# DeltaNet with a low-rank mixer on one core: the first batch's recurrence takes U into PSUM, its z goes through ScalarE, and the written-out order is new from there

## The chip, the core and the metric

The kernel runs on one core of a Trainium2 chip. Five engines work side by side, each through its own queue and in order: TensorE (PE) multiplies matrices into the accumulation memory PSUM, VectorE (DVE) and ScalarE (ACT) work elementwise and bring PSUM back into SBUF, GpSimd (POOL) clears tiles and issues some transfers, SyncE (SP) issues the others. Semaphores join them. The metric is the device time of one launch in microseconds, lower is better, as the median of several runs.

## The reference

Two blocks follow each other. The first is a delta rule, for 4 batches, 8 heads, 768 tokens and head size 48:

```python
k_n = k / (norm(k) + 1e-06)
for t in range(S):
    y[t]  = q[t] @ state
    v_old = state.T @ k_n[t]
    state = state + beta[t] * outer(k_n[t], v[t] - v_old)
```

The second takes the heads side by side as x (4 x 768 x 384):

```python
u   = x + (x.T @ U @ V).T              # over the tokens, rank 32
out = u + relu(u @ w_ch1) @ w_ch2      # 384 -> 1536 -> 384
```

U and V of this second block are weights. The U of the change is another thing: a term of the first block, below.

## The kernel before

The recurrence is not run token by token. A batch is cut into 12 chunks of 64 tokens, and six chunks make a unit n, so that batch b has units 2b and 2b + 1 and there are eight units. For each unit the kernel builds Gram matrices of k and q (`grams`, with `turn`, `placed` and `products`), inverts a triangular system by substitution on VectorE (`blocks`, steps of L842 and L848), and joins the small inverses into 64 x 64 ones on TensorE (`joins`, `part`, `diagonals`). Units 0 and 1 use a form with a halved substitution and larger joining matmuls (L899, L913).

With the inverse T of a chunk the recurrence over the chunks is short. Let S be the state, K the chunk's keys. Then U = T V holds the corrected values without the state, W = T K the corrected keys, z = U - W S, the output is y = Q S + (masked Q K) z, and the next state is S + K z. `prepare(n, h)` makes W for three chunks. `recur(b)` runs the twelve chunks in turn: one group of matmuls for W S (called b), z, one group for K z (s), and the addition to S on VectorE (L1214, L1216 for the first chunk). `outputs` makes y in two groups (L1024 and L1038) and copies it to X (L1008).

There are two ways to make z, and the constant JOINT chooses by batch. For b < JOINT, `prepare` also multiplies U (L1083), copies it to SBUF (L1096), and z is the subtraction U - W S on VectorE, out of PSUM (L1182). For b >= JOINT, `prepare` copies W with its sign turned, a part `values(c)` multiplies U of one chunk into a pair of PSUM banks, the group b adds -W S into the same place, and ScalarE copies the sum as z (L1160). The other half of that pair later takes the product for the next state. JOINT is 1, so that only batch 0 goes the first way.

The weights come as 64-bit floats, in 14 slices numbered 0 to 13. SyncE starts each slice as two transfers (`start`), ScalarE scales its upper words (`raised`, L1301), and VectorE puts the 32-bit numbers together in three steps (`load_weights`, L1315, L1322, L1329). The staging buffers are reused, so that a later slice starts only when an earlier one has been decoded.

When all chunks of batch 0 have their outputs, `front` makes u in strips of 256 tokens (L1574, L1580, L1588, L1593, L1609, L1621), `channels` multiplies by w_ch1 (L1683), and `narrow` by w_ch2 (L1861). From there on the mixer of one batch runs beside the preparation and the recurrence of the next.

All these parts are generators, and each `yield op(...)` is a step. What stands next on which queue is not left to a scheduler: ORDER, a text of some 2,500 numbers, lists for each part the positions of its steps, and `run` resumes the parts in this order. An engine's queue holds its own steps in order of their positions. Costs given to `op` decide nothing here.

For the steps that follow it matters where they stand. Before the change, with positions of ORDER: `recur b0` runs from 244 (the matmuls of the first state) to 474; `prepare n0 h1` stands at 211 to 223, `prepare n0 h0` at 227 to 233, `prepare n1 h0` at 356 to 369 and `prepare n1 h1` at 370 to 402; the joining steps of unit 1 lie between 232 and 335; the scalings of slices 6 to 13 stand at 363, 381, 384, 415, 432, 507, 505 and 575; the first `channels` step stands at 546. The names s0 to s10 below are the state additions of chunks 0 to 10 of batch 0, z1 to z11 its z.

Of the kernel before, what the change touches and what calls it, by code (L numbers as in the profile page):

```python
# [27 lines left out]
def kernel(  # L28
# [33 lines left out]
    NU = 2  # L62
# [82 lines left out]
    add_up b0 i0 f00: 607 626 632; add_up b0 i0 f03: 613 616 625; add_up b0 i1 f00: 858 866 891; add_up b0 i1  # L145
    f03: 853 867 874; add_up b0 i2 f00: 1070 1075 1083; add_up b0 i2 f03: 1094 1098 1102; add_up b1 i0 f00: 1305
    1309 1322; add_up b1 i0 f03: 1303 1316 1328; add_up b1 i1 f00: 1487 1488 1500; add_up b1 i1 f03: 1486 1497
    1501; add_up b1 i2 f00: 1708 1711 1720; add_up b1 i2 f03: 1709 1721 1723; add_up b2 i0 f00: 1859 1861 1863;
    add_up b2 i0 f03: 1860 1862 1864; add_up b2 i1 f00: 1999 2003 2012; add_up b2 i1 f03: 2002 2008 2011; add_up
    b2 i2 f00: 2224 2225 2227; add_up b2 i2 f03: 2226 2228 2230; blocks n0: 61 73 75 76 82 84 86 88 89 91 93 94  # L150
    96 97 103 110 114 122; blocks n1: 143 157 160 163 173 175 179 192 201 206 208 212 213 215 218 219 226 229;
    blocks n2: 479 509 512 515 517 519 521 528 532 535 538 540 543 545 549 551 554 558; blocks n3: 648 661 678
    680 682 693 701 706 707 716 717 721 725 734 736 738 749 753 755 760 763 770 771 773 787 788 789 790 799 801
    810 811 812 813; blocks n4: 957 971 973 974 975 986 988 990 991 998 1003 1005 1018 1019 1030 1057 1065 1069
    1071 1073 1076 1078 1082 1084 1085 1088 1090 1097 1099 1103 1108 1117 1129 1133; blocks n5: 1164 1187 1195
    1199 1218 1223 1226 1249 1258 1262 1276 1286 1291 1304 1307 1318 1330 1335 1337 1345 1347 1352 1358 1362
    1368 1372 1374 1380 1382 1389 1391 1403 1404 1410; blocks n6: 1535 1560 1566 1569 1577 1578 1579 1595 1596
    1597 1610 1611 1624 1630 1632 1647 1657 1665 1668 1672 1674 1687 1697 1707 1726 1728 1731 1738 1745 1748
    1751 1764 1773 1779; blocks n7: 1829 1853 1868 1869 1870 1873 1875 1884 1893 1895 1898 1901 1905 1909 1920
    1925 1926 1936 1937 1946 1950 1956 1969 1972 1975 1988 1994 1996 2000 2004 2014 2015 2020 2022; channels b0  # L160
    i0 e0: 546 547; channels b0 i0 e1: 556 557; channels b0 i0 e2: 562 563; channels b0 i0 e3: 565 566; channels
    b0 i0 e4: 580 582; channels b0 i0 e5: 599 601; channels b0 i1 e0: 708 709; channels b0 i1 e1: 727 741;
    channels b0 i1 e2: 754 756; channels b0 i1 e3: 758 781; channels b0 i1 e4: 797 807; channels b0 i1 e5: 808
    837; channels b0 i2 e0: 987 989; channels b0 i2 e1: 1000 1001; channels b0 i2 e2: 1020 1025; channels b0 i2
    e3: 1053 1054; channels b0 i2 e4: 1061 1062; channels b0 i2 e5: 1079 1087; cut f0 f00 k0 to1: 2338; cut f0
    f00 k1 to0: 2316; cut f0 f00 k1 to1: 2333; cut f0 f00 k2 to0: 2347; cut f0 f00 k2 to1: 2361; cut f1 f03 k0
    to1: 2369; cut f1 f03 k1 to0: 2429; cut f1 f03 k1 to1: 2372; cut f1 f03 k2 to0: 2409; cut f1 f03 k2 to1:
    2418; cut f2 f06 k0 to1: 2325; cut f2 f06 k1 to0: 2362; cut f2 f06 k1 to1: 2337; cut f2 f06 k2 to0: 2346;
    cut f2 f06 k2 to1: 2357; cut f3 f09 k0 to1: 2395; cut f3 f09 k1 to0: 2416; cut f3 f09 k1 to1: 2396; cut f3
    f09 k2 to0: 2417; cut f3 f09 k2 to1: 2421; diagonals n0 h0: 188 190 191 195 210 222; diagonals n0 h1: 167  # L170
    169 171 176 181 186; diagonals n1 h0: 312 315 319 336 343 353; diagonals n1 h1: 290 292 303 338 349 358;
    diagonals n2 h0: 628 649 660 667 686 696; diagonals n2 h1: 665 684 689 711 723 730; diagonals n3 h0: 820 821
    830 833 841 842; diagonals n3 h1: 878 905 907 908 925 956; diagonals n4 h0: 1153 1163 1166 1197 1244 1245;
    diagonals n4 h1: 1216 1231 1233 1267 1287 1289; diagonals n5 h0: 1416 1421 1433 1434 1435 1440; diagonals n5
    h1: 1450 1505 1537 1555 1556 1587; diagonals n6 h0: 1823 1890 1891 1913 1914 1915; diagonals n6 h1: 1843
    1872 1878 1889 1906 1911; diagonals n7 h0: 2041 2055 2071 2080 2112 2121; diagonals n7 h1: 2044 2048 2078
    2139 2144 2151; fifteen b1 i0 k0: 1176 1181 1186 1212 1232 1243 1274; fifteen b1 i0 k1: 1160 1178 1183 1211
    1225 1240 1256 1273; fifteen b1 i1 k0: 1394 1398 1406 1426 1455 1464 1468; fifteen b1 i1 k1: 1371 1396 1402
    1420 1431 1448 1458 1465; fifteen b1 i2 k0: 1581 1598 1613 1628 1639 1662 1675; fifteen b1 i2 k1: 1576 1588
    1605 1614 1631 1640 1654 1670; fifteen b2 i0 k0: 1762 1777 1789 1805 1820 1832 1848; fifteen b2 i0 k1: 1758  # L180
    1765 1778 1803 1806 1819 1830 1847; fifteen b2 i1 k0: 1921 1933 1953 1962 1967 1979 1984; fifteen b2 i1 k1:
    1910 1930 1934 1951 1961 1964 1978 1983; fifteen b2 i2 k0: 2088 2111 2135 2146 2163 2198 2213; fifteen b2 i2
    k1: 2089 2119 2130 2145 2162 2166 2178 2190; front b0 i0: 495 497 504 511 526 537; front b0 i1: 542 555 614
    629; front b0 i2: 845 859 862 863; front b1 i0: 1060 1077 1080 1089 1095 1114; front b1 i1: 1265 1275 1313
    1315; front b1 i2: 1478 1480 1499 1506; front b2 i0: 1688 1694 1699 1710 1724 1735; front b2 i1: 1839 1854
    1866 1888; front b2 i2: 1945 1948 2007 2029; front b3 i0: 2214 2215 2216 2219 2221 2229; front b3 i1: 2232
    2233 2237 2238; front b3 i2: 2240 2242 2245 2246; gather b0 i0 h0 c0 k0: 623; gather b0 i0 h0 c0 k1: 633;
    gather b0 i0 h0 c1 k6: 705 934; gather b0 i0 h1 c0 k2: 655; gather b0 i0 h1 c0 k5: 715 1171; gather b0 i0 h1
    c1 k3: 666; gather b0 i0 h1 c1 k4: 681; gather b0 i1 h0 c0 k0: 876; gather b0 i1 h0 c0 k1: 911; gather b0 i1
    h0 c1 k6: 970 1126; gather b0 i1 h1 c0 k2: 920; gather b0 i1 h1 c0 k5: 964 977; gather b0 i1 h1 c1 k3: 919;  # L190
    gather b0 i1 h1 c1 k4: 942; gather b0 i2 h0 c0 k0: 1100; gather b0 i2 h0 c0 k1: 1109; gather b0 i2 h0 c1 k6:
    1169 1609; gather b0 i2 h1 c0 k2: 1131; gather b0 i2 h1 c0 k5: 1159 1321; gather b0 i2 h1 c1 k3: 1135;
# [486 lines left out]
    def grams(n, i):  # L679
# [46 lines left out]
        def products(j, i):  # L726
# [3 lines left out]
            for c in range(UC):  # L730
                for par, g in QUADS:
# [5 lines left out]
                        start=True,  # L737
# [256 lines left out]
    JOINT = 1  # L994

    def recur(b):
# [127 lines left out]
        zs = {}  # L1124
        if b >= JOINT:
            for c in range(NC):
# [992 lines left out]
```

## Time and profile before

| | |
|---|---|
| median of 3 runs | 579.35 us (577.87 to 580.1) |
| the profiled execution | 579.14 us, its span 577.4 us |
| TensorE busy | 544.6 us, 94% of the span |
| VectorE busy | 466.7 us, 81% |
| ScalarE busy | 252.0 us, 44% |
| GpSimd busy | 133.5 us, 23% |
| mean granted clock of TensorE | 0.939 |
| moved by DMA | 36.26 MB |

The times to predict are medians of unprofiled runs. The profile is one execution; its span runs from the first to the last instruction, and 1.7 us of the execution's own time lie around it. A row of a timeline gives the start, the time taken, the engine, the line, the operation, and what is written from what, in what size; "x16" is the number of merged instructions, and a bracket at the end the idle time before it and what ended it. Each fp32 matmul of the program stands as two instructions. The granted clock is the share of TensorE's full clock that the chip gave it. The matmuls overlap, so that the distance from start to start is what a group costs on the queue, not its length.

### The profile page before, as it was taken

To read this page: it belongs to the slowest core of one execution; us is meant where nothing else is said; L and a number is where in the kernel's file an instruction comes from. 1 tells how busy PE (TensorE), PEld (TensorE's weight loads), DVE (VectorE), ACT (ScalarE), POOL (GpSimd) and SP (SyncE) were. 2 spreads that over 40 slices of the span, in tenths; PEclk is the share of its full clock that TensorE was granted. 3 is DMA by queue.
4 is the path that set the end of the run, shared out by engine and by line. 5 is a ranking of instruction groups with operands and counts; after the bars stand their busy time and mean duration, and the time that the engine had idled before them with its cause. 6 is when DMAs were issued, how large, how long until landed. Compare 5 with 4: busy or idle time off the path is not lost.

```text
span 577.4 us, 24113 instructions
## 1 busy us (share of the span) xinstructions
PE 544.6 (94%) x10692; PEld 482.3 (84%) x10692; DVE 466.7 (81%) x1100; ACT 252.0 (44%) x528; POOL 133.5 (23%) x229
## 2 busy tenths in 40 slices
PE   3878888899999999999999999999999999999997
PEld 3777876588988986998999998989999978755996
DVE  3888768899999789999996799989995435799942
ACT  2846565644435542266154643264345461345000
POOL 9122026205124430072222262061002000000000
PEclk9665557999999999999999999999999999999999
DMA  9980628643022243131501523060003000000001
GB/s 144 182 183 26 221 69 196 140 85 65 20 51 43 48 77 63 30 85 36 98 10 20 102 58 82 2 128 19 3 2 85 5 3 1 28 0 1 1 27 69
DMA packets 89399, 36.26 MB, mean 63 GB/s; under 512 B 75408, under 2 KB 87056, under 8 KB 89296
## 3 DMA queue, kind: packets, MB, share of 16 engines
q1 hardware_dynamic: 80752, 24.69, 20.7%
q0 software_dynamic: 6944, 9.74, 7.9%
q8 instruction: 84, 1.38, 1.0%
q10 hardware_dynamic: 1600, 0.30, 0.3%
q14 instruction: 19, 0.16, 0.1%
HBM read 29.98 MB, written 4.72 MB: 60 GB/s over the span
## 4 chain that ended last, share of the span: by engine, by line
PE 83%; DVE 7%; ACT 4%; issue 2%; DMA 2%; SPq 1%; DVEq 0%; ACTq 0%
PE P L1861 21%; PE P L1721 15%; PE P L1683 9%; PE P L1988 7%; PE P L1488 7%; PE P L733 3%; PE P L1024 2%; PE P L1114 2%; PE P L1146 2%; PE P L913 2%; PE P L1064 2%; PE P L1038 2%; PE P L899 2%; PE P L1609 1%; PE P L1588 1%
## 5 line engine op out<-in xcount | busy, mean ns | idle before, releaser
L1861 PE MATMUL P<-w_sb,hs 128*128 128x192 f32 x540 | 94.4, 329 | 0.0
L1861 PEld LDWEIGHTS P<-w_sb,hs 128*128 128x128 f32 x540 | 87.2, 190 | 2.6 <-issue 1.8
L848 DVE TENSOR_TENSOR xt<-xt,prod 128x112 f32<-128x112 f32 (+21 forms) x200 | 64.6, 323 | 6.9
L842 DVE TENSOR_TENSOR prod<-gs,xt 128x112 f32<-128x112 f32 (+21 forms) x200 | 62.8, 314 | 2.2
L1721 PE MATMUL P<-S,w_sb 128*128 128x128 f32 x432 | 56.6, 282 | 0.0
L1721 PEld LDWEIGHTS P<-S,w_sb 128*128 128x128 f32 x432 | 51.5, 191 | 2.6 <-DVE xt L848 0.6
L1683 PE MATMUL P<-ut,w_sb 128*128 128x256 f32 x216 | 51.4, 388 | 0.0
L1750 DVE TENSOR_TENSOR hs<-hs,P 128x512 f32<-128x512 f32 x54 | 36.5, 682 | 11.8 <-PE P L1721 10.4
L1683 PEld LDWEIGHTS P<-ut,w_sb 128*128 128x128 f32 x216 | 39.6, 190 | 7.4 <-issue 1.8
L588 POOL DMA_DIRECT2D slot<-in_v_dram x32 | 21.2, 669 | 102.2 <-DVE X L1788 46.8
L1008 ACT COPY X<-P 64x192 f32<-64x192 f32 x96 | 30.0, 313 | 22.0 <-PE P L1038 19.4
L985 POOL MEMSET slot<- 32x384 f32 x32 | 13.1, 412 | 107.6 <-PE P L942 101.9
L1160 ACT COPY z<-P 128x192 f32<-128x192 f32 x36 | 11.4, 318 | 60.4 <-PE P L1146 52.1
L1861 PE MATMUL P<-w_sb,S 128*128 128x192 f32 x216 | 37.7, 329 | 0.0
L1861 PEld LDWEIGHTS P<-w_sb,S 128*128 128x128 f32 x216 | 34.9, 190 | 0.8 <-issue 0.6
L978 ACT COPY slot<-zz 32x384 f32<-32x384 f32 x64 | 32.3, 509 | 4.3 <-DVE zz L917 3.3
L1744 ACT ACTIVATE hs<-P 128x512 f32<-128x512 f32 x30 | 17.8, 597 | 36.5 <-PE P L1721 32.9
L733 PE MATMUL P<-slot 48*64 48x64 f32 x1536 | 30.9, 233 | 0.7 <-DVE slot L770 0.7
L588 POOL DMA_DIRECT2D slot<-in_k_dram x44 | 29.7, 678 | 7.9 <-PE P L1202 7.6
L733 PEld LDWEIGHTS P<-slot 48*64 48x64 f32 x1536 | 27.7, 146 | 4.0 <-issue 1.5
L574 POOL DMA_DIRECT2D slot<-in_k_dram x40 | 24.6, 622 | 11.3 <-PE P L1202 6.5
L1214 DVE TENSOR_TENSOR s<-s,P 128x192 f32<-128x192 f32 x40 | 14.0, 349 | 14.7 <-PE P L1202 10.9
(208 smaller groups left out, 1197.4 us busy)
## 6 DMA issues: line engine op xcount, KB each, us to landing
w_sb<-in_moe_w_ch_dram SPq DMA_DIRECT2D x10, 384.0 KB, 5.4
out_dram<-X SPq DMA_DIRECT2D x19, 192.0 KB, 2.8
slot<-in_k_dram SPq DMA_DIRECT2D x48, 72.0 KB, 3.5
slot<-in_k_dram POOLq DMA_DIRECT2D x44, 72.0 KB, 3.4
slot<-in_v_dram SPq DMA_DIRECT2D x32, 72.0 KB, 3.1
slot<-in_v_dram POOLq DMA_DIRECT2D x32, 72.0 KB, 2.9
X<-in_moe_w_ch_dram SPq DMA_DIRECT2D x6, 384.0 KB, 5.0
wide<-in_moe_w_ch_dram SPq DMA_DIRECT2D x6, 384.0 KB, 5.7
```

The source lines that it names most:

```text
L588: queue.dma_start(out=t[half(1 - g if name == "z" else g), :, to, 0:D], in_=src[b, 4 * g + s, hf * UC * L : (hf + 1) * UC * L, :].rearrang ...
L733: nc.tensor.matmul(p_g[half(g ^ (par * i)), par, c], kq[rows, c, j, 0, half(g)], kq[rows, c, j, i, half(g)], start=True, stop=True,)
L842: nc.vector.tensor_tensor(out=prod, in0=gb[:, :, j : j + 1, j + 1 :].to_broadcast([128, split, m, w]), in1=xb[:, :, 0:m, j : j + 1].to_bro ...
L848: nc.vector.tensor_tensor(out=xb[:, :, 0:m, j + 1 :], in0=xb[:, :, 0:m, j + 1 :], in1=prod, op=ALU.subtract,)
L978: nc.scalar.copy(pg[quarter(i), :, at, :, a : a + BK], cut(zc, h)[quarter(i)].rearrange("p r (c j) t -> p r c j t", j=2),)
L1008: nc.scalar.copy(x[half(c % 2), c // 2, 4 * D * g : 4 * D * (g + 1)].rearrange("p (j r d) -> p r j d", r=2, d=D), states(p_y)[half(g)],)
L1488: nc.tensor.matmul(to, forms[h][w][:, g] if isinstance(w, str) else w1_of(*w, h)[:, g], TOKENS[t] if isinstance(t, str) else u_of(*t), sta ...
L1683: nc.tensor.matmul(p_f[:, x], w(x, t), ut[:, t], start=(t == 0), stop=(t == KT - 1))
L1721: nc.tensor.matmul(p[:, g], forms[h][w][:, g % 2] if isinstance(w, str) else w1_of(*w, h)[:, g % 2], PLACES[int(t[1:])] if isinstance(t, s ...
L1750: nc.vector.tensor_tensor(out=to, in0=to, in1=p, op=ALU.add if sign > 0 else ALU.subtract)
L1861: nc.tensor.matmul(to, of[0], of[1], start=of[2], stop=of[3], skip_group_check=True)
L1988: nc.tensor.matmul(p[:, m], a[:, h, 128 * m : 128 * m + 128], v[:, h, j], start=fresh and h == j == 0 and (m == 0 or apart), stop=(j == h ...
```

## The change

JOINT becomes 0, so that batch 0 too goes the second way: `values` for its twelve chunks, the b group added into PSUM, z copied by ScalarE. Two conditions in `products` that were written with JOINT keep their meaning as plain numbers (n > 2 and n <= 2; before, NU * JOINT was 2).

```diff
@@ products @@
-                if n > NU * JOINT:
+                if n > 2:
...
-                for r in range(2) if n <= NU * JOINT else ():
+                for r in range(2) if n <= 2 else ():
@@ ahead of recur @@
-    JOINT = 1
+    JOINT = 0
```

ORDER has five steps more: `values b0` brings twelve, `recur b0` one (the z of the first chunk), and the four `prepare` of units 0 and 1 lose two each. Up to position 204 it is as before. From 205 to 1097 it is new: other positions for nearly all parts, those of batch 0's recurrence, unit 1's joins, the weight slices, units 2, 3 and the beginning of 4, batch 0's mixer and batch 1's recurrence. From 1098 on (1093 before) it is the former one with all numbers five higher. The positions that the prediction speaks of, in place of the full text:

```diff
-prepare n0 h0: 227 228 231 233; prepare n0 h1: 211 214 221 223
-prepare n1 h0: 356 366 368 369; prepare n1 h1: 370 376 394 402
+prepare n0 h0: 230 235; prepare n0 h1: 234 239
+prepare n1 h0: 351 360; prepare n1 h1: 412 422
+values b0 c0 to c11: 229 237 263 290 318 332 366 385 395 405 423 463
-joins n1 h0: 254 267 279 284 287 293 295 297 298 307 308 313 325 327 328 335
-joins n1 h1: 232 234 236 239 247 258 268 271 281 285 286 289 302 304 305 324
+joins n1 h0: 228 253 254 255 269 270 275 276 277 283 284 289 291 293 296 300
+joins n1 h1: 231 249 259 260 304 307 313 319 324 340 341 342 378 390 397 399
-recur b0: 244 249 250 264 266 270 273 283 300 306 310 316 322 331 332 337 342
-  344 347 348 362 365 371 373 374 377 378 387 396 399 404 405 410 413 417 424
-  426 429 436 445 463 465 471 474
+recur b0: 236 241 242 256 257 265 268 272 288 303 306 308 316 320 333 336 343
+  349 350 355 367 369 377 382 383 393 394 396 400 402 407 409 413 419 426 429
+  433 437 440 441 446 465 466 470 484
-load_weights, from the fourth: 225 241 245 251 255 269 272 282 288 291 301 311
-  330 333 339 364 375 379 392 401 409 422 425 430 431 433 439 450 452 508 516
-  518 520 530 552 560 581 585 597
+load_weights, from the fourth: 232 243 245 246 271 274 278 279 280 301 302 305
+  314 325 344 345 348 352 358 368 375 384 386 387 391 404 406 408 417 420 425
+  439 456 458 459 460 489 527 542
-raised i3 to i13: 262 278 320 363 381 384 415 432 507 505 575
+raised i3 to i13: 252 264 298 330 335 359 379 398 418 455 483
-products n2 i0 (first steps): 449 455; turn n2 i0: 440 443
+products n2 i0 (first steps): 468 490; turn n2 i0: 450 464
-outputs b0 c0: 240 253 259 ... outputs b0 c11: 466 476 480 481
+outputs b0 c0: 238 240 250 ... outputs b0 c11: 469 496 497 498
-front b0 i0: 495 497 504 511 526 537; channels b0 i0 e0: 546 547
+front b0 i0: 502 506 519 520 522 530; channels b0 i0 e0: 531 532
```

In `recur b0` before, the numbers are in turn PE and VectorE for the first chunk (s, the copy of the state), and then b, z, s, addition for each further one. After, the first chunk has z, s, copy, and each further one b, z (now ScalarE), s, addition. In `joins` of unit 1 the second, third, fifth and sixth numbers are the diagonal steps, the 10th, 11th, 13th and 14th the off-diagonal ones on PE.

On SyncE's queue the starts of slices 3 and 4 go ahead of unit 1's v, and the later slices ahead of the loads of unit 2's k and q. On GpSimd's queue two loads of unit 1's v (209, 210) go ahead of two clearings of unit 0 (214, 215; before, 210 and 222).

More of the change, by code (lines that the diff above doesn't have):

```diff
@@ L180 @@
[L180 to L189, printed above, removed]
```

460 lines of the change are left out of this document (236 added, 224 removed).

## The prediction

> **What bounds the kernel now.** I read the page first, then the stretches of 4 us, then who waited for whom between 44 and 116 us, then single instructions. The page gives busy time and share of the span for TensorE (PE) and VectorE (DVE), the granted clock in 40 slices of 14.4 us, and the chain that ended last:
>
> ```profile
> PE 544.6 (94%) x10692; PEld 482.3 (84%) x10692; DVE 466.7 (81%) x1100; ACT 252.0 (44%) x528; POOL 133.5 (23%) x229
> PEclk9665557999999999999999999999999999999999
> PE 83%; DVE 7%; ACT 4%; issue 2%; DMA 2%; SPq 1%; DVEq 0%; ACTq 0%
> ```
>
> PE is busy for 94% and carries the chain, and its clock is low only in the first seven slices. The stretches (from:to, length, then busy us of PE, PEld, DVE, ACT, POOL, the granted clock, DMA share, GB/s) show where it still idles:
>
> ```profile
> 36.00:40.00 4.00, 4.00 (x80) 4.00 (x79) 3.26 (x9) 1.82 (x5) 0.54 (x1) 0.50 1.11 219
> 68.00:72.00 4.00, 2.74 (x64) 2.74 (x66) 0.16 (x1) 1.15 (x3) 0.00 (x0) 0.50 0.73 243
> 84.00:88.00 4.00, 3.76 (x164) 3.60 (x156) 0.88 (x2) 3.90 (x8) 2.81 (x5) 0.58 0.43 91
> 88.00:92.00 4.00, 2.65 (x143) 2.27 (x136) 3.62 (x8) 2.98 (x5) 3.40 (x6) 1.00 0.92 169
> 96.00:100.00 4.00, 3.54 (x71) 2.91 (x64) 3.93 (x6) 2.17 (x5) 3.75 (x7) 0.50 0.94 196
> 116.00:120.00 4.00, 4.00 (x21) 3.51 (x20) 3.71 (x15) 0.65 (x2) 0.00 (x0) 1.00 0.89 220
> ```
>
> From 116 us PE is full at full clock. There a new order of the same matmuls can only lose. What the edit can gain lies between about 50 us and the mixer's first matmul (L1683 below), where PE has gaps and mostly half clock. The anchors there are DVE's copies of the state S: s0 (L1216), s4 and s5 (L1214), s10 (L1214). After them come the front's copy (L1580) and the first mixer matmul (columns: start, us, engine, line, operation):
>
> ```profile
> 59.84 0.34 DVE L1216 COPY s<-P 128x192 f32<-128x192 f32 x1
> 80.49 0.35 DVE L1214 TENSOR_TENSOR s<-s,P 128x192 f32<-128x192 f32 x1
> 85.92 0.34 DVE L1214 TENSOR_TENSOR s<-s,P 128x192 f32<-128x192 f32 x1
> 103.66 0.34 DVE L1214 TENSOR_TENSOR s<-s,P 128x192 f32<-128x192 f32 x1
> 109.07 0.56 DVE L1580 COPY tt<-P 128x384 f32<-128x384 f32 x1
> 114.46 2.86 PE L1683 MATMUL P<-ut,w_sb 128*128 128x256 f32 x12
> ```
>
> **The change, part by part.** First its arithmetic, by groups (all of the span for L1160, 48 to 116 us for the others):
>
> ```profile
> L1160 ACT COPY z<-P 128x192 f32<-128x192 f32 x36 | 11.4, 318 | 60.4 <-PE P L1146 52.1
> L1182 DVE TENSOR_TENSOR z<-slot,P 128x192 f32<-128x192 f32 x11 | 3.8, 348 | 4.7 <-PE P L1169 4.3 <-ACT X L1008 0.4
> L1096 ACT COPY slot<-P 128x576 f32<-128x576 f32 x4 | 2.6, 638 | 0.6 <-PE P L1083 0.6
> L1083 PE MATMUL P<-slot 64*64 64x48 f32 x192 | 5.7, 277 | 0.0
> L957 PE MATMUL P<-zz 32*32 32x32 f32 x72 | 2.6, 238 | 2.0 <-ACT X L1008 1.1 <-ACT zz L947 0.9
> ```
>
> - DVE loses 11 subtractions, 3.8 us. ScalarE (ACT) gains 12 z copies of 318 ns, 3.8 us, and loses four copies of U, 2.6 us. One z on the chain costs 318 instead of 348 ns: 0.03 us times 11, nothing.
> - PE loses the U products of prepare (192 matmuls, 5.7 us) and gains twelve groups of the same 16 matmul rows each, `values`. Below I price a group at 0.46 us, which gives 5.5 us. Equal. The minus sign rides on a copy that is there anyway, and the conditions n > 2 and n <= 2 decide as before. Cost nil.
> - One pair of PSUM banks per chunk now serves z and S, held from `values` on, where two were taken. Nothing in the trace prices it; I take 0, with at most one 0.7 us wait (such as those of the front below) as an upper end and none as the lower.
>
> So the work is equal, and the order decides. I price PE's queue between s0 and s10 in both orders with these rows of the half clock, and two rows of full clock (102.82, 103.04) for comparison:
>
> ```profile
> 64.16 0.70 PE L1169 MATMUL P<-s,slot 48*64 48x48 f32 x16
> 64.62 0.66 PE L1038 MATMUL P<-z,slot 64*64 64x48 f32 x16
> 65.08 1.43 PE L899 MATMUL P<-zz,hs 64*64 64x16 f32 x24
> 97.94 1.54 PE L705 MATMUL P<-ident,slot 128*128 128x128 f32 x6
> 101.12 1.89 PE L733 MATMUL P<-slot 48*64 48x64 f32 x96
> 102.82 0.40 PE L1024 MATMUL P<-s,slot 48*64 48x48 f32 x16
> 103.04 0.36 PE L1202 MATMUL P<-z,slot 64*48 64x48 f32 x16
> ```
>
> From start to start a group of the recurrence (b, S, both halves of y, `values`) is 0.46 us, at full clock 0.22. A diagonal step of unit 1's joins is 1.43, an off-diagonal one 0.4 (six in the L957 row's 2.6 us), a half of prepare 1.4 (5.7 over 4), a turning 1.5, a product 0.95 (1.89 over 2). PE's queue from s0 to s10 then sums to:
>
> - before: 4.2, 8.4, 3.4, 2.6, 3.7, 4.2, 3.2, 1.4, 1.8 and 7.2, together 40.1 us. The trace has 103.66 - 59.84 = 43.8, so 3.7 us are waits.
> - after: 7.6, 6.8, 5.2, 3.1, 3.7, 3.1, 1.8, 3.7, 2.3 and 5.8, together 43.1 us. All eight diagonal steps of unit 1 now follow s0 (two went ahead of it), and ten `values` groups lie between; against that two U products and two products of unit 2 have left. So **+3.0**.
>
> **s0 itself.** In DVE's queue the first state copy is passed by two steps of the weight decoding, of about 1.0 us each. PE's queue ahead of it is shorter by more. I take **-1.0**, between 0 and -2.0. On POOL two loads of unit 1's v go ahead of two clearings of the first unit, but within time in which POOL waits anyway. The three rows before z are one weight's decoding, 2.48 us from 97.61 to 100.09:
>
> ```profile
> 97.61 0.55 DVE L1315 TENSOR_SCALAR w_sb<-power 128x768 int32<-128x768 int32 x1
> 98.19 0.96 DVE L1322 SCALAR_TENSOR_TENSOR w_sb<-X,w_sb 128x768 int32<-128x768 int32 x1
> 99.18 1.03 DVE L1329 SCALAR_TENSOR_TENSOR w_sb<-X,w_sb 128x768 uint16<-128x768 uint32 x1
> 100.09 0.35 DVE L1182 TENSOR_TENSOR z<-slot,P 128x192 f32<-128x192 f32 x1
> ```
>
> **Waits that go, and those that stay** (columns: us in total, times, longest):
>
> ```profile
> PE P L913 <- issue: 1.5, 1, 1.5
> PE P L1024 <- DVE s L1214: 1.2, 2, 0.7
> PE P L1609 <- DVE X L1593: 0.7, 1, 0.7
> PE P L1588 <- DVE tt L1580: 0.7, 1, 0.7
> DVE w_sb L1315 <- ACT X L1301: 2.9, 1, 2.9
> ```
>
> DVE stood 2.9 us for the scaling of weight 6, with s5 queued behind it: s4 to s5 took 5.43 us against 3.7 in PE's queue. The new order has that scaling long before, so **-1.7**. The 1.5 us with no releaser I leave in. PE's waits for S stay: the copy is as long, and z takes 0.03 less.
>
> **From s10 to the mixer.** Two products (1.89 us) now stand behind s10, ahead of the front; a turning and a product fill the two waits of 0.7 for tt and X. **+0.5**.
>
> **The clock.** Before, three of unit 1's four prepare products ran on each other's heels, and the stretch 88 to 92 had clock 1.00:
>
> ```profile
> 82.94 1.52 PE L1064 MATMUL P<-slot 64*64 64x64 f32 x48
> 86.31 1.36 PE L1064 MATMUL P<-slot 64*64 64x64 f32 x48 [0.24 <-DVE s L1214]
> ```
>
> Now one product stands there, and the other half's comes three chunks later. If the stretch is lost, some 13 groups cost 0.46 instead of 0.22, 3.1 us. But the chunks there run at the pace of the chain S, b, z more than of PE (2.65 of 4.00 busy in 88 to 92). I take **+0.8**, between 0 and 3.1.
>
> **The sum**: 3.0 - 1.0 - 1.7 + 0.5 + 0.8 = +1.6 us. The profiled execution took 579.14 us (span 577.4 and 1.7 around it), 0.2 under the median of 579.35. Against the median the sum gives 580.9; I forecast **580.9, no change that counts**, and set the rivals against the median too. A difference under 0.5% (2.9 us) is about what a measurement of this kernel can't tell from none.
>
> **The rivals.**
>
> *Slower: the full-clock stretch is lost and nothing covers it.* The clock term is 3.1, not 0.8: 580.9 + 2.3 = 583.2 us. For it: clock 0.50 and 0.58 around that stretch. Against it: PE idled a third of it. It decides once every stretch from s0 to s10 stays at 0.50 and PE is busy over 3.5 of 4 us in those of s5 to s9. 0.22.
>
> *Slower: late weights hold z.* ACT works in order, and now z, not only the decoding, queues behind the scalings of weights 8 to 13 (positions 359 to 483). Landing:
>
> ```profile
> w_sb<-in_moe_w_ch_dram SPq DMA_DIRECT2D x10, 384.0 KB, 5.4
> wide<-in_moe_V_dram SPq DMA_DIRECT2D x4, 192.0 KB, 8.9
> ```
>
> Weight 11's buffer is free shortly before s5, and its scaling stands right behind the z of chunk 8, some 6.9 us later by the queue: 1.5 us to spare at 5.4, 2.0 too late at 8.9. Weight 12 has 2.7 to spare and would be 0.8 late. Together 2.8, hence 583.7 us. The point is a landing above 6.9. 0.16.
>
> *Faster: the gaps close.* PE runs its 43.1 us with no other wait and keeps a full-clock stretch: s10 at 58.84 + 43.1 - 3.1 = 98.8 instead of 103.66, 4.9 less, plus the 0.5 behind it: 575.0 us. For it: the decoding moves up into idle DVE time (0.16 busy of 4.00 in 68 to 72), and the queue past s10 holds no decoding for long. Against: two thirds of the 3.7 us are waits inside the chain. 0.18.
>
> *Faster: the clock rises early.* With PE dense between s0 and s3 the clock may be 1.00 from there on. PE's 43.1 us shrink by half, and DVE's queue bounds: twelve decodings of 2.5 us, ten S, about 4 us of other work, 37 us: s10 near 95.9, 7.8 less, plus 0.5: 572.1 us. Against: the stretch 36 to 40 was busy 4.00 of 4.00 at clock 0.50. 0.05. [...]
>
> The rest, 0.03, is a new gap behind 116 us.
>
> **How the numbers follow.** No change 0.36; slower 0.22 + 0.16 + 0.03 = 0.41; faster 0.18 + 0.05 = 0.23. The forecast is the likeliest case, its own range 577 to 582.2. The range for all goes from the closing gaps, less the bounds of s0, to late weights plus a lost clock stretch: 573 to 587.
>
> **What would show it.** Right: twelve z copies of about 318 ns on ACT before 110 us, no L1182, L1083 or L1096 at all; s1 some 7.6 us after s0; s4 to s5 near 3.7; s10 at 103 to 106; the first L1683 at 114 to 118; full PE from there. Wrong: a granted clock other than 0.50 from s0 to s9, ACT waits at L1301 with z behind them, or PE waits after the first L1683.

## The result, and the profile after

The changed kernel takes 586.44 us (median of 4 runs, 584.68 to 588.03) where the kernel before took 579.73 (577.87 to 581.28) beside it: a ratio of 1.0116, with a 95% interval of 1.0072 to 1.0161. It is slower by 6.7 us. The profiled execution has a span of 583.6 us, 6.2 more than before.

First the page of the changed kernel: busy time of TensorE, ScalarE and VectorE, the granted clock in 40 slices of 14.6 us, and the chain that ended last by engines.

```profile
PE 547.2 (94%) x10692; PEld 485.3 (83%) x10692; DVE 464.8 (80%) x1089; ACT 252.8 (43%) x536; POOL 133.3 (23%) x229
PEclk9755556799999999999999999999999999999999
PE 86%; ACT 4%; DVE 4%; issue 3%; DMA 1%; SPq 0%; DVEq 0%; ACTq 0%
```

The work is nearly the same. In the chain, VectorE's share went from 7% to 4%; its subtractions, 3.8 us in all, can be only a small part of that. "issue", time for which the profile has no releaser, went from 2% to 3%. Lines below the order text stand two lower in the changed kernel: the group for W S is L1148, `values` L1116, z on ScalarE L1162, s L1204, the additions to S L1218 (first) and L1216, the raise of a weight piece L1303.

Now the anchors of the prediction in the timeline of the changed kernel: VectorE's s0, s1, s4, s5, s7, s8, s9 and s10, the front's copy, and the first mixer matmul.

```profile
57.96 0.35 DVE L1218 COPY s<-P 128x192 f32<-128x192 f32 x1
61.51 0.34 DVE L1216 TENSOR_TENSOR s<-s,P 128x192 f32<-128x192 f32 x1
...
79.61 0.35 DVE L1216 TENSOR_TENSOR s<-s,P 128x192 f32<-128x192 f32 x1 [0.81 <-PE P L1204]
84.01 0.35 DVE L1216 TENSOR_TENSOR s<-s,P 128x192 f32<-128x192 f32 x1 [0.62 <-PE P L1204]
...
90.25 0.35 DVE L1216 TENSOR_TENSOR s<-s,P 128x192 f32<-128x192 f32 x1 [0.18 <-PE P L1204]
95.94 0.35 DVE L1216 TENSOR_TENSOR s<-s,P 128x192 f32<-128x192 f32 x1 [0.33 <-PE P L1204]
101.33 0.35 DVE L1216 TENSOR_TENSOR s<-s,P 128x192 f32<-128x192 f32 x1 [4.17 <-PE P L1204]
108.95 0.35 DVE L1216 TENSOR_TENSOR s<-s,P 128x192 f32<-128x192 f32 x1 [2.17 <-PE P L1204]
116.45 0.56 DVE L1582 COPY tt<-P 128x384 f32<-128x384 f32 x1
120.83 4.37 PE L1685 MATMUL P<-ut,w_sb 128*128 128x256 f32 x19
```

Of before, the prediction does not show s7:

```profile
91.51 0.35 DVE L1214 TENSOR_TENSOR s<-s,P 128x192 f32<-128x192 f32 x1 [0.34 <-ACT slot L1096]
```

Against the same rows of before, the loss can be laid out stretch by stretch:

| stretch | before, us | after, us | difference |
|---|---|---|---|
| start to s0 | 59.84 | 57.96 | -1.88 |
| s0 to s7 | 31.67 | 32.29 | +0.62 |
| s7 to s10 | 12.15 | 18.70 | **+6.55** |
| s10 to the first mixer matmul | 10.80 | 11.88 | +1.08 |
| sum | 114.46 | 120.83 | +6.37 |

The sum is the whole difference of the two spans (6.2 us). At s7 the changed kernel is still 1.26 us ahead; three chunks later it is 5.29 behind. So the question is what happens between 90 and 109 us. The waits of TensorE between 56 and 118 us (total, times, longest):

```profile
PE P L1116 <- issue: 5.0, 2, 3.0
PE P L1026 <- issue: 1.5, 2, 1.1
PE P L959 <- issue: 1.1, 1, 1.1
PE P L941 <- issue: 0.8, 1, 0.8
PE P L735 <- ACT z L1162: 0.7, 1, 0.7
PE P L1040 <- issue: 0.6, 1, 0.6
```

Nine us of waits have no releaser, against 2.1 before (of which the prediction quoted the largest, 1.5). The profile shows no semaphore that would end them. The three largest, in the timeline:

```profile
92.75 0.56 PE L1116 MATMUL P<-slot 64*64 64x48 f32 x10 [2.01 <-issue]
99.50 0.38 PE L1116 MATMUL P<-slot 64*64 64x48 f32 x10 [2.96 <-issue]
106.03 0.34 PE L1026 MATMUL P<-s,slot 48*64 48x48 f32 x2 [1.12 <-issue]
```

They sum to 6.1 us, and all lie between s7 and s10, where the kernel before had 0.3 us of such waits. So they are 5.8 of the 6.55 us; the other waits are 1.4 us fewer there, and beside all waits TensorE runs 2.2 us longer (12.4 instead of 10.2 us, at a granted clock of 0.59 instead of 0.72). The stretches of 4 us of the changed kernel show what else is special there (columns as in the prediction; the last two are the DMA share and GB/s):

```profile
88.00:92.00 4.00, 2.45 (x76) 1.99 (x68) 3.75 (x6) 1.99 (x5) 2.41 (x4) 0.50 1.27 185
92.00:96.00 4.00, 3.25 (x124) 3.25 (x124) 1.72 (x4) 1.90 (x3) 2.29 (x4) 0.50 1.18 197
96.00:100.00 4.00, 1.04 (x46) 0.88 (x44) 1.16 (x2) 0.66 (x3) 2.94 (x5) 0.87 1.14 271
100.00:104.00 4.00, 3.66 (x95) 3.19 (x87) 1.30 (x2) 2.33 (x6) 0.94 (x2) 0.55 1.20 193
104.00:108.00 4.00, 2.88 (x40) 2.36 (x38) 2.54 (x3) 1.26 (x3) 0.00 (x0) 0.50 0.30 42
```

From 88 to 104 us TensorE is busy for 10.4 of 16 us (before, 12.6) and the DMA share stands at 1.14 to 1.27. Before, it stood at 0.86 to 0.96 there. (The share is the summed time of the packets over that of 16 engines; it can pass 1.) What has been added is small packets. For the window 88 to 104 us the DMA view of the changed kernel says:

```profile
DMA packets 6186, 3.38 MB, mean 211 GB/s; under 512 B 4838, under 2 KB 5988, under 8 KB 6182
```

And that of the kernel before:

```profile
DMA packets 4925, 3.41 MB, mean 213 GB/s; under 512 B 3385, under 2 KB 4745, under 8 KB 4921
```

The same bytes, but 1,450 more packets under 512 bytes. These are loads of the third and fourth unit (rows of 192 bytes, and blocks of 128 and 64 bytes), which fall together with weight pieces. By the packet records the rows of 192 bytes took a share of 0.39 there and 0.20 before, and the weight pieces' packets of 1,536 bytes 0.42 and 0.46.

Instructions come by DMA too. The table of DMA queues on the page of the changed kernel has a queue of kind "instruction" with 84 packets:

```profile
q8 instruction: 84, 1.38, 1.0%
```

The records give each packet 16,384 bytes. TensorE has 10,692 matmuls, as many weight loads and 87 instructions of its sequencer in the trace, 21,471 in all or 255.6 for each packet. So I read a packet as a lot of 256 of TensorE's instructions. If that is right, a wait for instructions can stand only where a lot begins. It does. I number TensorE's instructions in order of their start, and take the remainder by 256. The six waits without a releaser over 0.5 us of the changed kernel, worked out from the records:

```
the wait ends at, us             68.25   77.90   82.45   92.75   99.50  106.03
remainder of the number            193     193     193     194     194     194
packet before it landed at, us   66.94   76.43   81.17   91.14   98.16  104.69
from landing to the end, us       1.31    1.47    1.28    1.61    1.34    1.34
```

In the 14 profiles of this study TensorE has 55 waits without a releaser between 56 and 118 us. All 55 end at such a number (193 or 194), and 1.25 to 1.71 us after an instruction packet has landed. I take them for waits for instructions. No lot of any profile begins sooner than 1.2 us after its packet has landed.

A fetch starts (in 164 of 168 cases between 55 and 113 us) after TensorE has begun the lot before the one that is fetched. The table gives, for the lots around the loss, when TensorE ran the first instruction of a lot, how long after that the fetch of the next one started, and the DMA share in that time (worked out from the records; the expectations below give 3.0, 5.4 and 5.2 us for the three late ones, by a rougher count that puts two of the beginnings inside waits):

```
before:  81.8  0.7 (0.00)   85.4  1.1 (0.49)   89.1  2.0 (0.94)   93.6  1.3 (1.05)   97.9  1.9 (0.89)
after:   82.5  1.4 (0.00)   86.3  3.4 (1.03)   92.8  4.3 (1.11)   99.5  3.7 (1.17)  106.0  1.4 (0.06)
```

A packet of the changed kernel takes 0.9 to 1.6 us, and at least 1.2 us pass from its landing to the first instruction. In the kernel before, the lots begin 3.6 to 4.5 us after one another there (81.8 to 97.9), so that a fetch which starts after 3.4 to 4.3 us, as in the changed kernel, comes too late. What makes the fetches late is the theory that the experiments had to test.

### The profile page after: what moved, and what is told of

Its sections match the earlier page's. It is cut to its first block, busy times and chain, and to the rows that moved or that the text cites. A ratio compares the mean times of both kernels' runs of the same rounds, so it can differ in the third digit from the quotient of the medians.

```text
span 583.6 us, 24083 instructions
## 1 busy us (share of the span) xinstructions
PE 547.2 (94%) x10692; PEld 485.3 (83%) x10692; DVE 464.8 (80%) x1089; ACT 252.8 (43%) x536; POOL 133.3 (23%) x229
## 4 chain that ended last, share of the span: by engine, by line
PE 86%; ACT 4%; DVE 4%; issue 3%; DMA 1%; SPq 0%; DVEq 0%; ACTq 0%
PE P L1863 21%; PE P L1723 14%; PE P L1685 8%; PE P L1990 7%; PE P L1490 7%; PE P L735 4%; PE P L1116 3%; PE P L1026 3%; PE P L1066 2%; PE P L1148 2%; PE P L1040 2%; PE P L915 2%; PE P L901 2%; PE P L1204 2%; PE P L1611 1%
## 5 line engine op out<-in xcount | busy, mean ns | idle before, releaser
L1752 DVE TENSOR_TENSOR hs<-hs,P 128x512 f32<-128x512 f32 x54 | 36.5, 682 | 11.6 <-PE P L1723 10.2
L1162 ACT COPY z<-P 128x192 f32<-128x192 f32 x48 | 15.2, 318 | 67.0 <-PE P L1148 49.9
L829 POOL MEMSET xt<- 128x1056 f32 x8 | 7.9, 985 | 116.0 <-DVE zz L857 115.9
L1216 DVE TENSOR_TENSOR s<-s,P 128x192 f32<-128x192 f32 x40 | 14.0, 350 | 25.3 <-PE P L1204 20.7
L1116 PE MATMUL P<-slot 64*64 64x48 f32 x768 | 26.0, 242 | 5.3 <-issue 5.2
```

What stands on the lines that cost most here:

```text
L1116: nc.tensor.matmul(states(pair(x)[:, :, 0 : 2 * D])[half(g ^ par), par, j], zt[half(g), par, cu, j], vn[half(g), cu, 2 * par + j], start=( ...
L1752: nc.vector.tensor_tensor(out=to, in0=to, in1=p, op=ALU.add if sign > 0 else ALU.subtract)
```

## The experiments

The theories, as numbered in the expectations. Theory 1: loads on the DMA engines delay TensorE's instruction lots, and the new order puts loads and a dense stretch of small matmuls together. Theory 2: late weight pieces hold z in ScalarE's queue (a rival of the prediction). Theory 3: the code itself costs, not the order. Theory 4: the half clock between s5 and s10 is most of the loss (the other slower rival). Theory 5: TensorE's queue sets the time, whatever the clock. Theory 6: the stalls belong to the new order of TensorE's instructions, whatever the DMAs do.

**The two halves of the change, each alone.** The order of before with the new code, and the new order with the old code; steps that were not ready at their place were taken as soon as they were.

```diff
 e1, against the order of before
-prepare n0 h0: 227 228 231 233
+prepare n0 h0: 226 229; values b0 c0: 225; values b0 c1: 242; values b0 c2: 264
...
-recur b0: 244 249 250 264 266 270
+recur b0: 240 243 248 249 263 266 270
 e2, against the new order
-values b0 c0 to c11: 229 237 263 290 318 332 366 385 395 405 423 463
-prepare n0 h0: 230 235; recur b0: 236 241 242 256 257 265
+prepare n0 h0: 229 230 235 237; recur b0: 242 243 257 258 265
```

> The new code of the first batch (U added up in PSUM, z copied by ScalarE) on the old order of steps: the halves that are gone are dropped, each group of U is put behind the copy of the z before it, and the first z is put ahead of the first s; nothing else is moved. Theory 1 (what costs is where the new order puts weight pieces 11 to 13 and the loads of the next units, so that TensorE waits for its own instructions between s7 and s10): the loads stand where they stood, so about the time of before, 578 to 582 us, with unreleased TensorE stalls of at most 3 us between 44 and 130 us. Theory 3 (what costs is the code itself: the values spread out over the recurrence, ScalarE in the loop): 584 to 588 us.

> The old code of the first batch (U as a block beside the solved keys, z subtracted by VectorE) on the new order of steps: the values' steps are dropped, each prepared half gets its two more steps beside the ones it has. Theory 1 (the order of loads starves TensorE's instruction supply): 584 to 588 us, with unreleased TensorE stalls of some 6 us between s7 and s10. Theory 3 (the code itself): about the time of before, 578 to 582 us.

Measured: the code alone 589.88 us (ratio 1.0161, 1.0127 to 1.0194), the order alone 588.12 (1.0124, 1.0085 to 1.0164). Each half alone costs at least as much as both together (for the order alone the intervals overlap), so neither theory's pair of numbers came out. The traces differ. With the code alone, the stalls without a releaser are 1.7 us between s0 and the front, as theory 1 expects, but something else took their place. ScalarE's timeline in e1:

```profile
98.42 0.31 ACT L1010 COPY X<-P 64x192 f32<-64x192 f32 x1
104.49 0.89 ACT L1303 ACTIVATE X<-wide 128x768 f32<-128x768 f32 x1 [5.75 <-DMA wide<-in_moe_w_ch_dram]
105.41 0.96 ACT L1010 COPY X<-P 64x192 f32<-64x192 f32 x3
106.39 0.80 ACT L722 COPY slot<-P 128x768 f32<-128x768 f32 x1
107.09 0.33 ACT L1162 COPY z<-P 128x192 f32<-128x192 f32 x1
```

A raise waits 5.75 us for its weight piece, and z of chunk 10 stands behind it. s9 is added at 99.59, s10 only at 112.79. This is theory 2 on the old order: z on VectorE had been out of the way of the raises. The new order raises the pieces in time. With the order alone, the lots are late (3.0 us of stall at the prepared U products, 4.6 in all) and z and the state additions wait on VectorE for TensorE and TensorE for them (7.8 us on VectorE).

**The loads alone.** TensorE's order was kept (in e4 but for two turns of the third unit); the steps of the loads and the weight pieces were moved.

```diff
 e3, against the new order (first positions)
-start i11: 415 416; start i12: 453 454; start i13: 472 477; raised i11 to i13: 418 455 483
+start i11: 426 457; start i12: 473 474; start i13: 532 542; raised i11 to i13: 516 515 581
-load n2 k: 424 428 431 432; load n3 b: 500 507 508 509
+load n2 k: 390 391 394 396; load n3 b: 483 484 485 486
 e4, against the order of before: the reverse
-start i11: 423 458; start i12: 475 477; start i13: 533 553; load n2 k: 389 390 393 397
+start i11: 412 413; start i12: 452 453; start i13: 475 479; load n2 k: 418 422 425 426
```

> The changed kernel with its loads and its weight pieces alone (start, raise and decode) put back, relative to the steps of the recurrence, the front and the channels, to where the old order has them; TensorE's own order is that of the changed kernel, step for step. Theory 1: the fetches of instructions come every 4 to 5 us again between s7 and s10, the unreleased stalls fall from 9.2 us to 3 us or less, and the time to 578 to 582 us. Theory 2 (the late pieces of weights hold z back in ScalarE's queue): also some us faster, but with the waits on ScalarE's raises gone and the unreleased stalls still there. Theory 3: 585 to 588 us, as the changed kernel.

> The kernel before with its loads and its weight pieces alone moved, relative to the steps of the recurrence, the front and the channels, to where the new order has them; TensorE's steps stay as they are but for two turns of the third unit, which wait for its keys. Theory 1: unreleased TensorE stalls of some 6 us appear between s7 and s10 and the time goes to 583 to 587 us. Theory 3: 578 to 582 us, as before.

Measured: e3 603.70 us (1.0383, 1.0334 to 1.0431), e4 590.47 (1.0167, 1.0134 to 1.0201). The expectation for e3 missed. Its first mixer matmul came at 121.68, no sooner than in the changed kernel; the DMA share from 88 to 104 us was still 1.11, and the stalls fell only from 9.0 to 6.7 us (the other 20 us were lost after that point and were not followed up). The place in the order did not decide alone when a load ran: the third unit's k left SyncE's queue at 85.3 us in the changed kernel and at 85.6 in e3, and loads from two queues met again in the same stretch. e4 is slower than either theory had it: between s0 and the front it has 3.5 us of stalls, not 6, but TensorE waits 6.1 us for VectorE and 4.6 for ScalarE too. These two show that the position of the loads costs much, not that the instruction lots are the way by which it does.

**Fewer weights in the stretch.** The three last pieces go behind the last z.

```diff
 e7, against the new order
-start i11: 415 416; start i12: 453 454; start i13: 472 477; raised i11 to i13: 418 455 483
+start i11: 469 470; start i12: 472 473; start i13: 505 506; raised i11 to i13: 487 511 560
```

> The changed kernel with weight pieces 11, 12 and 13 (start, raise, decode: 1.2 MB of the 4.2 MB that land between 84 and 104 us) put behind the last z of the first batch; the loads of the third and fourth unit stay. TensorE's order is that of the changed kernel. Theory 1 (TensorE's instruction fetches queue behind the weight loads): the unreleased stalls fall from 9.0 us between s0 and tt to 4 us or less, and s10 comes 4 to 6 us earlier, 104 us or less, with the time at 579 to 583 us. Theory 6 (the stalls are where TensorE's instructions run out, whatever the DMAs do): the stalls stay within 2 us of 9.0 and the time within 2 us of the changed kernel's 586.

Measured: 593.89 us (1.0240, 1.0209 to 1.0272). The time is slower than either expectation, and the stalls lie between the two: they fell to 5.6 us and s10 came at 108.24, s7 to s10 in 15.49 instead of 18.70 us, but the DMA share from 88 to 104 us was still 1.10, with the small packets of the units. From s10 to the first mixer matmul it takes 16.56 us instead of 11.88, of which TensorE waits 2.1 for the front's copy; that the late weights' decoding holds it is likely but not shown. Another 5.5 us are lost behind that point and were not followed up. Undecided.

**The clock.** Products of the identity with itself, into PSUM columns that nothing reads, add array work ahead of s.

```diff
+                    at_s = sums[c + 1]
...
+                for _ in range(4 if b == 0 and c > 3 else 0):
+                    nc.tensor.matmul(pair(at_s)[:, 0, 384:512], ident, ident, start=True, stop=True, skip_group_check=True)
                 for j, par, g in heads:
```

In e8 it is `6 if b == 0 else 0`. In e5 and e8 these products, with start=True, go into the bank in which U is being added up, and the output is not the same any more (relative error 0.25 and 0.33); the time is read, not the result. In e6 the bank holds no sum.

> The changed kernel with four products of the identity with itself (128x128 by 128 columns, into columns of the PSUM banks that nothing reads) put on TensorE ahead of the s products of chunks 4 to 10: 28 products, which at the 0.200 us of a turn's matmul (4.8 us for 24 turns in the profile of before) are 5.6 us more of TensorE's queue at half clock, and a part of them falls into waits. Theory 4 (the granted clock of a stretch of 3.41 us follows the array work of the stretch before it, rows times columns times streamed columns, and half clock in s5 to s10 is most of the loss): the stretches from s5 on rise over the bound, TensorE gets the full clock from about 85 to 90 us on, the stretch s4 to the tail's first tt shrinks by 2 us or more against the changed kernel, and the time falls to 578 to 585 us. Theory 5 (the queue of TensorE sets the time, and the clock only follows): 2 to 6 us slower than the changed kernel, 588 to 592 us.

> The kernel before with the same 28 products at the same places (ahead of the s products of chunks 4 to 10). Theory 4: its two full-clock stretches from 87 us on join the one from 101 us, and the time falls by 0 to 4 us, to 576 to 580 us. Theory 5: 2 to 6 us slower, 582 to 586 us.

> The changed kernel with six such products ahead of every s product of the first batch, 66 in all: 13.2 us of TensorE's queue at half clock, 6.6 at full. Theory 4: the full-clock stretch that opens at s0 (56 us) is held, the granted clock between s0 and s10 is mostly full, the small matmuls of the recurrence take less, and the time is 577 to 586 us in spite of the added work. Theory 5: 6 to 13 us slower than the changed kernel, 592 to 599 us.

Measured: e5 592.93 us (1.0218, 1.0179 to 1.0257), e6 587.97 (1.0148, 1.0107 to 1.0190), e8 592.18 (1.0234, 1.0198 to 1.0270). All three are at or above the numbers of theory 5. Yet these totals don't decide, for the expectations priced a product at half its cost: the 0.2 us of a turn's matmul are those of one instruction, and a product of the identity is two. By the trace the 28 products of e5 hold TensorE's queue for 10.1 us, those of e6 for 9.4, and the 60 of e8 behind s0 for 19.0, while the way from s0 to the front grew by only 3.9, 4.5 and 4.3 us. The rest went into shorter stalls and into the clock. (In e6 the first s already stood 2.4 us later than before, ahead of all added products; that part of its 8.6 us is not explained. In e5, 5.4 us were lost behind the first mixer matmul.) The stretches of 4 us of e8:

```profile
88.00:92.00 4.00, 3.45 (x122) 3.01 (x123) 3.20 (x5) 3.37 (x7) 3.96 (x6) 1.00 0.78 236
92.00:96.00 4.00, 3.68 (x136) 3.26 (x134) 2.83 (x5) 1.02 (x4) 2.79 (x5) 1.00 1.28 148
96.00:100.00 4.00, 3.39 (x108) 2.96 (x107) 2.72 (x4) 2.15 (x4) 3.47 (x5) 1.00 1.21 186
100.00:104.00 4.00, 1.00 (x56) 0.75 (x48) 1.22 (x2) 0.62 (x2) 1.86 (x3) 1.00 1.09 236
```

The clock could be raised: it is 0.96 from 72 to 104 us, where the changed kernel has 0.55. s4 to s7 took 11.67 us, against 10.64 in the changed kernel, with 18 products more in it. Their 36 instructions in that stretch of e8 (busy time, then mean ns), and one group of six products with the matmuls behind it:

```profile
L1205 PE MATMUL P<-ident 128*128 128x128 f32 x36 | 4.8, 284 | 0.0
85.81 1.60 PE L1205 MATMUL P<-ident 128*128 128x128 f32 x12
87.34 0.40 PE L1208 MATMUL P<-z,slot 64*48 64x48 f32 x16
```

From start to start a group holds the queue for 1.53 us, three of them for 4.6. TensorE waits 1.0 us in either stretch, so that the rest of its queue, nearly the same matmuls in the same order (341 and 336 instructions), took 6.1 us at clock 1.00 and 9.6 at 0.50. The full clock is thus worth up to 3.5 us in these three chunks; how much of it the waits on ScalarE and VectorE would take back without the added products is not shown. And from 100 to 104 us TensorE stood idle at full clock for three quarters of the time, with the DMA share at 1.09: a wait of 3.8 us at the beginning of a lot. So the stalls come at full clock too. Theory 4 falls as the main cause, by the sum between s7 and s10 above (stalls 5.8 of 6.55 us, TensorE's longer running 2.2), and theory 5 falls with it: the queue takes much less time at full clock.

**The loads made light.** The cut that tells theory 1 from theory 6: the same transfers in the same order with the same waits, but for the third and fourth unit q, k, v, the shifted keys and the blocks bring only a sixth of their rows. These units then compute on what lay in the slot before.

```diff
+                few = 1 if n in (2, 3) else UC
                 queue.dma_start(
-                    out=t[half(1 - g if name == "z" else g), :, to, 0:D],
+                    out=t[half(1 - g if name == "z" else g), 0:few, to, 0:D],
...
-                        out=blocked(n)[quarter(y % 4), j, g, :, 0:w],
+                        out=blocked(n)[quarter(y % 4), j, g, 0 : UC * L // BK // (6 if n == 3 else 1), 0:w],
```

> The changed kernel with the loads of q, k, the shifted keys and the blocks of the third and fourth unit cut to a sixth of their rows (same transfers, same order, same waits; the rest of the slot keeps what lay there, so these units compute on data that isn't theirs); the weight pieces load in full. Every engine's order is that of the changed kernel. Theory 1 (a lot of 256 TensorE instructions, 16 KB, is fetched over the same DMA engines, and waits there behind the loads): the wait from the end of a lot to the next fetch, 3.0, 5.4 and 5.2 us at 87, 92 and 98 us, falls to 0.3 to 2 us, the unreleased stalls between s0 and tt from 9.0 to 3 us or less, s7 to s10 from 18.7 to 14 us or less, and the time to 577 to 582 us. Theory 6 (the stalls belong to the new order of TensorE's instructions itself): stalls stay at 7 us or more, and the time at 584 to 588.

> The kernel before with the same cut loads. Theory 1: it had only 2.1 us of unreleased stalls, so it gains 0 to 3 us, 576 to 580 us, and the gap between the two kernels shrinks from 6.7 to 3 us or less. Theory 6: the gap stays at 5 us or more.

Measured: the changed kernel 579.36 us (0.9975, 0.9944 to 1.0005, against the kernel before), the kernel before 578.70 (0.9970, 0.9949 to 0.9992). With light loads the gap between the two shrinks from 6.7 to 0.7 us. The stretches of 4 us of e9:

```profile
88.00:92.00 4.00, 3.53 (x107) 2.82 (x103) 3.19 (x6) 2.64 (x7) 0.71 (x2) 0.50 0.59 195
92.00:96.00 4.00, 4.00 (x168) 3.93 (x172) 3.76 (x6) 2.31 (x6) 4.00 (x8) 0.57 0.47 120
96.00:100.00 4.00, 3.34 (x142) 2.75 (x130) 2.96 (x6) 2.87 (x9) 0.93 (x2) 1.00 0.71 208
100.00:104.00 4.00, 2.85 (x113) 2.34 (x115) 3.09 (x5) 3.54 (x6) 0.00 (x0) 1.00 0.42 114
```

The largest waits of TensorE in e9 from 56 to 118 us (its lines stand one lower than those of the changed kernel):

```profile
PE P L942 <- issue: 1.9, 1, 1.9
PE P L902 <- DVE zz L858: 0.9, 1, 0.9
PE P L1041 <- issue: 0.9, 1, 0.9
```

VectorE's s7 and s10 in the timeline of e9:

```profile
93.12 0.35 DVE L1217 TENSOR_TENSOR s<-s,P 128x192 f32<-128x192 f32 x1 [0.17 <-PE P L1205]
...
103.36 0.36 DVE L1217 TENSOR_TENSOR s<-s,P 128x192 f32<-128x192 f32 x1
```

And the packets of e9 from 88 to 104 us:

```profile
DMA packets 2899, 2.55 MB, mean 159 GB/s; under 512 B 1326, under 2 KB 2894, under 8 KB 2894
```

s7 to s10 takes 10.24 us instead of 18.70, the stalls are 3.1 instead of 9.0, none of them between s7 and s10, and the fetches of the lots that TensorE begins at 89.2, 93.2 and 96.7 us start after 1.4, 0.8 and 0.8 us. Every engine's instructions stand in the order of the changed kernel. So theory 6 falls: the stalls come from the loads and not from the order of TensorE's instructions. s7 itself came 2.87 us later than in the changed kernel (a late lot at 78 us cost 1.9), so that s10 is 5.59 us earlier and the first mixer matmul, at 113.93 us, 6.90. The granted clock of e9 is 1.00 from 95.5 us on, with no product added; TensorE was busy for all 4.00 us from 92 to 96. Of the 8.46 us between s7 and s10, 6.1 are the stalls; TensorE runs 9.2 us instead of 12.4, at a granted clock of 0.89 instead of 0.59, and the other waits are 0.8 us more. The cut takes away bytes (3.38 to 2.55 MB) and packets (6,186 to 2,899) together; which of the two counts is not separated. In e10 the stalls between s0 and the front are 4.0 us, more than the 2.1 of before: 2.3 of them follow a fetch that started 3.1 us late at a DMA share of 0.89. Its median is 2 us lower all the same, though its profiled execution is not (span 577.9, before 577.4).

**One queue for the fourth unit's blocks.** An attempt at a version that keeps all data: eight of the sixteen small-packet loads go from POOL's queue to SP's.

```diff
-            if g and (n, name) != (0, "k"):
+            if g and (n, name) not in ((0, "k"), (3, "b")):
                 e = "pool"
```

> The changed kernel with the 16 loads of the fourth unit's key blocks (12x32 pieces of 128 or 64 bytes) all on SP's queue; before, eight of them go out on POOL's queue from 93.7 to 101.4 us while SP's queue loads too. Nothing is left out. Theory 1 (instruction lots are late while loads from two queues fill the DMA engines): the DMA share between 92 and 104 us falls below 1.1, the waits for the lots at 92 and 98 us shrink from 5.4 and 5.2 us to 2 to 4 us, the stalls by 2 to 5 us, the time to 581 to 585 us, unless the blocks that now land later (about 115 us) are waited for in the fourth unit. Theory 6: no change, 585 to 588 us.

> The kernel before with the same 16 loads all on SP's queue. Theory 1: its fetches wait 1 to 2 us there now and its unreleased stalls are 2.1 us, so little is to be had: 577 to 581 us, the same within 0.5 per cent, or some us slower if the blocks land too late.

Measured: e11 586.83 us (1.0094, 1.0073 to 1.0115), e12 580.98 (1.0000, 0.9982 to 1.0018). The first missed: the DMA share from 92 to 96 us was 1.28, and from 96 to 104 us 1.08 and 1.09, the fetches of the lots begun at 88.5, 94.7 and 101.7 us started after 3.1, 4.4 and 2.2 us, the stalls were 7.7 us. Queueing loads one behind the other did not empty the stretch. The second did as expected, with 3.5 us of stalls. No version was found that beats the kernel before.

What stays open: which of the moved steps lets the loads meet in the stretch. Neither putting back all loads (e3) nor moving the weights out (e7) nor one queue (e11) brought the share from 88 to 104 us under 1.1, and a run with only the order of SP's queue changed was not made.

## Why the prediction was right in its range and wrong in its reason

The time fell inside the range of 573 to 587, close to its slow end, but outside the likeliest case (580.9, own range 577 to 582.2). That it fell inside is luck: most of the loss comes from a term that the sum did not have. Step by step:

- **The arithmetic** held. ScalarE has twelve z copies of 318 ns before 116 us, and the groups of L1182, L1083 and L1096 are gone from VectorE, TensorE and ScalarE. No wait shows for the PSUM pairs.
- **s0** came 1.88 us sooner; taken 1.0, between 0 and 2.0.
- **TensorE's queue, +3.0.** Up to s7 it was priced at 31.3 us after and 29.7 before, and the trace has 32.29 and 31.67: +0.62 in place of +1.6. Within it the split was wrong: s1 came 3.55 us after s0, not 7.6, and the diagonal steps went into the next chunk (61.51 to 70.11). From s7 to s10 it was priced at 11.8 after and 10.4 before; TensorE ran 12.4 and 10.2 us there beside its waits.
- **The raise of weight 6, -1.7.** s4 to s5 took 4.40 us, not 3.7: a gain of 1.03 in place of 1.7.
- **s10 to the mixer, +0.5**: +1.08.
- **The clock, +0.8.** The full-clock stretch at 88 us was lost, as the first slower rival said, but not under its condition (every stretch at 0.50, TensorE busy over 3.5 of 4 us): TensorE was busy for 2.45 us from 88 to 92 and for 1.04, at 0.87, from 96 to 100. From s7 to s10 it ran 2.2 us longer, which holds the lost clock and the different queue together; e8 does not contradict the rival's price of 3.1, but the stalls, 5.8, are the larger part.
- **The step that failed** is the sentence "The 1.5 us with no releaser I leave in." It took a wait without a releaser for a constant of the kernel. I take it for a wait for instructions (it stands where a lot begins, 1.6 us after a packet landed, behind a fetch that started 3.5 us late at a DMA share of 1.03). Such waits went from 2.1 to 9.0 us in all, and with light loads beside them (e9) to 3.1. The prediction went through the change of SyncE's and GpSimd's queues for what lands when, and never asked what else travels with it, though the DMA share of 0.92 and 0.94 stood in its own rows.
- **The rival of late weights** was real and priced at the wrong place: the new order avoids it (ScalarE's raises in the changed kernel wait for no piece between s7 and s10), and on the old order it costs 5.75 us (e1).
- **The signs** "s10 at 103 to 106" and "first L1683 at 114 to 118" were missed, at 108.95 and 120.83; "full PE from there" held. The tail runs 6.4 us late, unchanged in length (462.8 us, before 463.0).

## What to carry to other kernels

A wait without a releaser on a queue of many small matmuls may be a wait for instructions; number the engine's instructions and see whether the waits stand at equal remainders, each shortly behind an instruction packet. All 55 did here, 1.25 to 1.71 us behind one. Look at the number of small packets in the same stretch before moving loads or matmuls there; at a DMA share over 1, 14 of 33 fetches started more than 3 us late in these profiles. And when a unit of work changes its engine, what it now queues behind has to be moved with it: z on ScalarE needed other times for the raises (5.75 us of waiting in e1). Last, price a test by the rows of its own instructions: here a product of two instructions was priced as one, and the times of three runs decided nothing.

## What the runs showed that was not expected

**Fetches of instruction lots started later at a high DMA share.** Over the 14 profiles, for 164 lots that TensorE began between 55 and 113 us and whose successor was fetched after that: with a DMA share under 0.5 in the wait the fetch started after 1.1 us in the median (0 of 67 over 3 us), at 0.5 to 1.0 after 2.1 us (9 of 64 over 3), above 1.0 after 2.3 us (14 of 33 over 3, the longest 5.6). With light loads (e9) the stalls of the changed kernel fell from 9.0 to 3.1 us.

**In these profiles the granted clock followed array work, not busy time.** The records of the clock change in steps of 3.413 us (kernel before: records of 3.41, 6.83, 10.24, 23.89, 27.31 and 474.45 us, and a last one of 4.02). Summing rows times columns times streamed columns of the matmuls in each such stretch, in units of one 128x128 product by one column (the fullest stretches at full clock have 4,100 to 4,400), the 14 profiles give for stretches at half clock:

```
array work of the stretch   stretches   next one at full clock
under 1200                      224              0
1200 to 1450                     36             10
1450 to 1700                     32             28
over 1700                        16             16
```

A matmul is counted where it starts; between 1,200 and 1,700 units both happened (38 of 68 were followed by full clock). Busy time does not tell: of 128 half-clock stretches with TensorE busy over 3.3 of 3.41 us, 42 were followed by full clock. The stretch from 36 to 40 us of the kernel before, busy throughout with small matmuls, has 256 units from 36.1 to 39.5 us and was followed by half clock.

**Full clock shortened the chunks' own queue by a third.** From s4 to s7 TensorE's own instructions of three chunks took 9.6 us at clock 0.50 and 6.1 at 1.00 (e8), though they are small matmuls in a chain with ScalarE and VectorE. What the whole kernel would gain by it no run shows, since the stalls stand in the way.
